# Retention with a mixture of adapters on one core: state per 64 tokens, another beginning, and deferred stores

## The chip, the core and the metric

The kernel runs on one core of one Trainium2 chip. The metric is the device time of one execution in microseconds (us). Times of "before" are from three runs; the profile is of one more execution.

## What is computed

`q`, `k` and `v` have the shape (8 batches, 8 heads, 576 positions, 64). Cut to what matters, the reference is

```python
scores = (1/8) * q @ k.T                         # per batch and head
Dmat = where(rel >= 0, gamma_h ** rel, 0)        # rel = query position - key position
x = (scores * Dmat) @ v                          # all heads side by side: 4608 x 512
logits = x @ w_gate                              # 8 experts
w = softmax of the 2 largest logits, 0 elsewhere
out = x + sum_e w[:, e] * (x @ A[e]) @ B[e]      # A[e]: 512 x 16, B[e]: 16 x 512
```

Because the decay is a power of the distance, `x` of a chunk of positions is the sum of the causal product within the chunk and of `q` times a state, the sum of `k` (outer) `v` over all earlier chunks. The kernel scales by powers of gamma on the key's side (table `gv`) and on the query's side (tables `gx`), so that the state needs no decay of its own.

## The kernel before

**Units.** A unit is 128 positions of two batches, with all heads. Four batches make a quad: four chunks of 128 for two pairs of batches, and one last unit of 64 positions of four batches, the tail unit. There are two quads, so 18 units, 0 to 17; units 8 and 17 are tail units. Units u and u+2 follow each other in the positions of one pair of batches.

**Products of a unit.** `T_mm` transposes k and q on TensorE, 16 products each (`pt_k`, `pt_q`; L248). The causal triangle of 128 positions is cut in halves of 64: `S0_mm` makes the scores of the first 64 keys against all 128 queries (16 products, N=128, L322), `S1_mm` those of the last 64 keys against the last 64 queries (16, N=64, L304). VectorE multiplies both with the triangle (`S0_mask`, `S1_mask`). `O_mm` (16 products, N=128, L432) multiplies a stacked weight W, which has v of the first 64 positions in one half of the partitions and the state in the other, with M, which stacks masked scores and q. `O1_mm` adds the last 64 keys (16, N=64, L451). `U_mm` makes the unit's own k (outer) v over its 128 positions (16 products, K=128, N=64, L395), and `U_out` adds the old state to it, half on VectorE and half on ScalarE and GpSimd (POOL).

**The adapters.** `xT_out` scales the output by `gx` on VectorE; `Z_mm` (8 products, N=136, L487) gives the projections on all A and the logits; `route_a`, `route_s` and `route_b` choose and weigh two experts on VectorE and ScalarE; `X_mm` turns the weighed projection (fp16, L587), `zT_out` copies it, `Y_mm` (L605) multiplies with B, `B_mm` (L620) adds x by transposing it back, `osb_out` copies the sum to `osb`, and `store` writes 2 x 256 KB.

**Order.** All order is written by hand: the order in the code is the order in each engine's queue. Units 0 and 1 and the start of unit 2 are written out. Then the loop `for r in range(2, END)` makes a round of unit r: U of r+1, O of r, scores of r+1, X of r-1, Z and routing of r, transposes of r+2, and Y, B and the store of r-1. Scaling k with `gv` (`k_scale`, L226), laying v into W (`W_values`) and turning q (`q_turn`) are POOL's.

**Loads.** q, k and v come as 2 x 256 KB a unit in runs of 256 bytes, all from the SP queue, except k of unit 0. `freed(u, nm)` issues the load that takes over the buffer of unit u; q has 3 buffers, k and v 4. The stores stand in the same queue, `store(r-1)` in round r; `osb` has 3 buffers.

Of the kernel before, what the change touches and what calls it, by code (L numbers as in the profile page):

```python
# [17 lines left out]
HALF = (LO, HI)  # L18
# [3 lines left out]
def kernel(  # L22
# [26 lines left out]

# [12 lines left out]
    tri3_np = np.stack([tri_np, np.ones((128, 64)), tri_np], axis=1)  # L62


    NG0 = 8
    g0_np = np.zeros((128, 2, HP, NG0), dtype=np.float32)
    gw = [w for w in (8, 16, 32, 64) if w >= NG0]
    gw_np = np.zeros((128, len(gw), 2, HP), dtype=np.float32)
    for hp in range(HP):
        for ho in range(2):  # L70
            g = gam[2 * hp + ho]
            g0_np[HALF[ho], 0, hp, :] = g ** -rows[None, :NG0]
            g0_np[HALF[ho], 1, hp, :] = scale * g ** rows[None, :NG0]
            for x, w in enumerate(gw):
                gw_np[HALF[ho], x, 0, hp] = g ** -float(w)
                gw_np[HALF[ho], x, 1, hp] = g ** float(w)
# [6 lines left out]
    dr_tri = nc.inline_tensor(tri3_np.astype(np.float32), "c_tri")  # L83
# [13 lines left out]
    pack = cpool.tile([128, 256], FP32, tag="pack", name="pack")  # L97
    g0, gws, gv, gc = (pack[:, ends[x] : ends[x + 1]] for x in range(4))
    g0 = g0.rearrange("p (t a i) -> p t a i", t=2, a=HP)
    gws = gws.rearrange("p (x t a) -> p x t a", x=len(gw), t=2)  # L100
    gv = gv.rearrange("p (c h) -> p c h", c=NCH)
    gc = gc.rearrange("p (c h) -> p c h", c=NCH - 1)
    tri3 = cpool.tile([128, 4, 64], FP32, tag="tri3", name="tri3")
    gkx = cpool.tile([128, 2, HP, 128], FP32, tag="gkx", name="gkx")
    gk = gkx[:, 0]
    gx = [gkx[:, 1]] + [
        cpool.tile([128, HP, 128], FP32, tag=f"gx{c}", name=f"gx{c}") for c in range(1, NCH)
    ]
# [27 lines left out]
    NBUF = {"q": 3, "k": 4, "v": 4}  # L136
# [43 lines left out]

    def copy(eng, out, in_):
        if eng is nc.scalar:
            nc.scalar.copy(out=out, in_=in_)  # L183
        else:
            eng.tensor_copy(out=out, in_=in_)  # L185
# [8 lines left out]
    def heads(tl, p):  # L194

        v4 = tl.rearrange("p (b a o) d -> p b a o d", b=2, o=2)
        return [v4[:, b, :, p ^ b, :] for b in range(2)]

    def W_open(u):
        n = 1 if full(u) else 2  # L200
        st[u]["W"] = [
            wk.tile([128, 2, 2, HP, Dh], FP32, tag=f"W{x}", name=f"W{x}", bufs=(5, 2)[x])
            for x in range(n)
        ]
        if units[u][0] == 0:
            for p in range(2):
                nc.gpsimd.memset(st[u]["W"][0][HALF[p], p], 0.0)

    def W_values(eng, u, ps=(0, 1)):
        vt = nat[("v", u)]  # L210
        for x, w in enumerate(st[u]["W"]):
            for p in ps:
                for b, src in enumerate(heads(vt[HALF[x]], p)):
                    copy(eng, w[HALF[1 - p], p, b], src)

    def V1_copy(eng, u):

        s = st[u]
        s["V1"] = wk.tile([64, 2, HP, Dh], FP32, tag="V1", name="V1", bufs=2)
        for b, src in enumerate(heads(nat[("v", u)][HI], 0)):  # L220
            copy(eng, s["V1"][:, b], src)

    def k_scale(eng, u, bs=slice(0, 2)):
        c = units[u][0]
        kt = nat[("k", u)].rearrange("p (b h) d -> p b h d", b=2)[:, bs]
        eng.tensor_tensor(  # L226
            out=kt, in0=kt,
            in1=gv[:, c, :].unsqueeze(1).unsqueeze(3).broadcast_to(
                (128, bs.stop - bs.start, H, Dh)
            ),  # L230
            op=ALU.mult,
        )

    def T_open(u, nm, tag):
        s = st[u]
        s["p" + nm] = bank(tag, [128, 2, HP, 2, 64], name=f"pt_{nm}")
        if nm == "q":
            s["M"] = wk.tile([128, 2, 2, HP, 128], FP32, tag="M", name="M", bufs=3)
            s["Qs"] = wk.tile([128, HP, 2, 64], FP32, tag="Qs", name="Qs", bufs=2)
        else:  # L240
            s["kT"] = wk.tile([128, 2, HP, 2, 64], FP32, tag="kT", name="kT", bufs=2)

    def T_mm(u, nm, bs=(0, 1)):
        src, ps = nat[(nm, u)], st[u]["p" + nm]
        for hp in range(HP):
            for b in bs:
                for r in range(2):
                    mm(  # L248
                        ps[:, r, hp, b, :],
                        lhsT=src[HALF[r], b * H + 2 * hp : b * H + 2 * hp + 2, :],  # L250
                        rhs=ident[HALF[r], 64 * r : 64 * r + 64],
                        is_transpose=True,
                        start=True,
                        stop=True,
                    )

    def q_out(eng, u, p):

        s = st[u]
        copy(  # L260
            eng,
            s["M"][HALF[p], p, 0].rearrange("p a (r i) -> p r a i", r=2),
            s["pq"][HALF[p], :, :, 0, :],
        )

    def qs_out(eng, u):

        s = st[u]
        copy(eng, s["Qs"].rearrange("p a r i -> p r a i"), s["pq"][:, :, :, 1, :])

    def q_turn(eng, u, p):

        s = st[u]
        copy(
            eng, s["M"][HALF[p], p, 1],
            s["Qs"][HALF[1 - p]].rearrange("p a r i -> p a (r i)"),
        )

    def k_out(eng, u, bs=slice(0, 2)):
        s = st[u]  # L280
        if bs == slice(0, 2):
            copy(
                eng, s["kT"].rearrange("p r a b i -> p (r a b i)"),
                s["pk"].rearrange("p r a b i -> p (r a b i)"),
            )
        else:
            copy(eng, s["kT"][:, :, :, bs.start, :], s["pk"][:, :, :, bs.start, :])


    def Q_of(u, b, ho, hp, sl):  # L290
        s = st[u]
        if b == 0:
            return s["M"][HALF[ho], ho, 0, hp, sl]
        return s["Qs"].rearrange("p a r i -> p a (r i)")[HALF[ho], hp, sl]

    def S1_mm(u, tag="R"):

        s = st[u]
        s["ps1"] = bank(tag, [128, 2, 512], name="ps1")
        for hp in range(HP):  # L300
            for b in range(2):
                for ho in range(2):
                    p = ho ^ b
                    mm(  # L304
                        s["ps1"][HALF[p], b, 64 * hp : 64 * hp + 64],
                        lhsT=s["kT"][HALF[ho], 1, hp, b, :],
                        rhs=Q_of(u, b, ho, hp, HI),
                        start=(hp == 0),
# [4 lines left out]
    def S0_mm(u, tag="S"):  # L313

        s = st[u]
        s["ps0"] = bank(tag, [128, 2, HP, 128], name="ps0")
        for hp in range(HP):
            for x, sl in ((0, slice(0, 128)),) if full(u) else ((0, LO), (1, HI)):
                for b in range(2):
                    for ho in range(2):  # L320
                        p = ho ^ b
                        mm(  # L322
                            s["ps0"][HALF[1 - p], b, hp, sl],
                            lhsT=s["kT"][HALF[ho], x, hp, b, :],
                            rhs=Q_of(u, b, ho, hp, sl),
                            start=(hp == 0 and x == 0),
# [4 lines left out]
    def S0b_mm(u, b, tag):  # L331

        s = st[u]
        s.setdefault("ps0b", {})[b] = bank(tag, [128, HP, 128], name="ps0")
        for hp in range(HP):
            for ho in range(2):
                p = ho ^ b
                mm(
                    s["ps0b"][b][HALF[1 - p], hp, :],
                    lhsT=s["kT"][HALF[ho], 0, hp, b, :],  # L340
                    rhs=Q_of(u, b, ho, hp, slice(0, 128)),
                    start=(hp == 0),
                    stop=True,
                    skip_group_check=True,
                )

    def S0b_mask(u, b):
        s = st[u]
        for p in range(2):
            sl = HALF[1 - p]  # L350
            m = tri3[sl, 0:2, :].rearrange("p t i -> p (t i)")
            nc.vector.tensor_tensor(
                out=s["M"][sl, p, b], in0=s["ps0b"][b][sl],
                in1=m.unsqueeze(1).broadcast_to((64, HP, 128)), op=ALU.mult,
            )

    def S1_mask(u):
        s = st[u]
        s["S1"] = wk.tile([128, 2, HP, 64], FP32, tag="S1", name="S1", bufs=2)
        nc.vector.tensor_tensor(  # L360
            out=s["S1"],
            in0=s["ps1"][:, :, 0 : 64 * HP].rearrange("p b (a i) -> p b a i", a=HP),
            in1=tri3[:, 0, :].unsqueeze(1).unsqueeze(1).broadcast_to((128, 2, HP, 64)),
            op=ALU.mult,
        )

    def S0_mask(u, p, bs=slice(0, 2)):
        s = st[u]
        sl = HALF[1 - p]
        n = bs.stop - bs.start  # L370
        if full(u):
            m = tri3[sl, 0:2, :].rearrange("p t i -> p (t i)")
            nc.vector.tensor_tensor(  # L373
# [720 lines left out]
```

## Time and profile before

| | before |
|---|---|
| median of three runs (lowest, highest) | 182.95 us (181.15, 183.76) |
| the profiled execution | 183.94 us |
| its span | 182.2 us |
| TensorE busy (its weight loads) | 173.1 us (157.8) |
| VectorE, ScalarE, GpSimd busy | 128.8, 76.3, 125.1 us |
| moved by DMA | 39.00 MB, 214 GB/s on the mean |
| from HBM, to HBM | 29.09 MB, 9.44 MB |

The span reaches from the first to the last instruction; the execution's time is 1.74 us longer. Busy times of different engines overlap. A row of a group reads: line, engine, operation, output and input tiles, shape, count, then busy time, mean ns of one, idle time ahead and what ended it.

### The profile page before, as it was taken

Reading aid. Unit: us, or ns where it says so; the run is one execution under the profiler, and the core shown is the slowest. Engines: PE = TensorE matmul, PEld = TensorE weight load, DVE = VectorE, ACT = ScalarE, POOL = GpSimd, SP = SyncE. Lnnn points to the kernel's source line nnn. Section 1 sums busy time; section 2 is a strip of 40 time slices with the busy share of each in tenths; the row PEclk is TensorE's granted clock in tenths of the full one; section 3 lists DMA queues with packets and bytes.
Section 4 is the critical chain, followed back from the end, with each engine's and each line's share of the span. In section 5 each row is a group of like instructions: output and inputs, shape, how many; then the busy total and the mean of one; then the engine's idle time right before and its main releaser. Section 6 shows DMA issues by size and latency. Waiting matters only on the chain.

```text
span 182.2 us, 9356 instructions
## 1 busy us (share of the span) xinstructions
PE 173.1 (95%) x4126; PEld 157.8 (87%) x4126; DVE 128.8 (71%) x232; ACT 76.3 (42%) x156; POOL 125.1 (69%) x214
## 2 busy tenths in 40 slices
PE   7998999599999999999999999999999999999980
PEld 6797998498999899998999999999999999989960
DVE  4494763718686869696868596969696969687770
ACT  0734164910707070706273634343444444443330
POOL 7396984998297959796987747858677777792000
PEclk9999999969999999999999999999999999999997
DMA  4999899899997979999989798989999999923125
GB/s 115 288 229 211 182 199 206 181 235 227 219 286 175 255 176 267 219 288 230 270 185 271 173 293 193 258 183 246 220 286 232 264 202 271 273 84 119 55 107 189
DMA packets 119368, 39.00 MB, mean 214 GB/s; under 512 B 114320, under 2 KB 114720, under 8 KB 119328
## 3 DMA queue, kind: packets, MB, share of 16 engines
q1 hardware_dynamic: 116480, 37.30, 82.9%
q10 hardware_dynamic: 2672, 0.96, 2.1%
q8 instruction: 32, 0.52, 1.1%
q0 software_dynamic: 176, 0.15, 0.5%
q14 instruction: 8, 0.07, 0.1%
HBM read 29.09 MB, written 9.44 MB: 212 GB/s over the span
## 4 chain that ended last, share of the span: by engine, by line
PE 87%; POOL 4%; DMA 3%; SPq 2%; DVE 0%; issue 0%; DVEq 0%
PE pz L487 18%; PE px L432 17%; PE pu L395 9%; PE ps L322 8%; PE pt_k L248 5%; PE px L451 5%; PE po L620 5%; PE pt_q L248 4%; PE po L605 4%; PE ps L304 4%; PE pf L723 3%; DMA v<-in_v_dram 3%; SPq L142 2%; PE pzt L587 2%; POOL sel L503 2%; PE pa L514 1%
## 5 line engine op out<-in xcount | busy, mean ns | idle before, releaser
L373 DVE TENSOR_TENSOR M<-ps,tri 64x1024 f32<-64x1024 f32 (+1 forms) x34 | 37.3, 1097 | 3.8 <-PE ps L322 3.1
L487 PE MATMUL pz<-AW,xT 128*128 128x136 f32 x288 | 37.7, 284 | 0.0
L226 POOL TENSOR_TENSOR k<-k,pack 128x1024 f32<-128x1024 f32 (+1 forms) x18 | 32.5, 1806 | 6.6 <-PE pt_k L779 2.9
L185 POOL COPY M<-Qs 64x512 f32<-64x512 f32 x36 | 21.9, 609 | 21.9 <-ACT Qs L183 16.1
L432 PE MATMUL px<-M,W 128*64 128x128 f32 (+1 forms) x640 | 36.1, 268 | 0.0
L185 POOL COPY W<-v 64x256 f32<-64x256 f32 x78 | 29.2, 395 | 10.0 <-DMA v<-in_v_dram 6.8
L487 PEld LDWEIGHTS pz<-AW,xT 128*128 128x128 f32 x288 | 34.6, 190 | 0.4
L183 ACT COPY kT<-pt_k 128x1024 f32<-128x1024 f32 x17 | 17.2, 1015 | 40.1 <-PE pt_k L248 40.1
L432 PEld LDWEIGHTS px<-M,W 128*64 128x64 f32 x640 | 32.8, 141 | 0.2
L470 DVE TENSOR_TENSOR xT<-px,gx 128x1024 f32<-128x1024 f32 x11 | 13.5, 1225 | 17.8 <-PE px L451 13.4
L185 DVE COPY osb<-po 128x1024 f32<-128x1024 f32 (+2 forms) x18 | 19.2, 1075 | 5.9 <-PE po L620 5.0
L596 ACT COPY zT<-pzt 128x256 f16<-128x256 f16 (+1 forms) x19 | 6.9, 361 | 37.7 <-PE pzt L587 37.7
L183 ACT COPY M<-pt_q 64x512 f32<-64x512 f32 x35 | 20.2, 577 | 1.8 <-DVE M L185 0.7
L395 PE MATMUL pu<-v,k 128*64 128x64 f32 x512 | 19.2, 229 | 1.6 <-DMA v<-in_v_dram 1.6
L395 PEld LDWEIGHTS pu<-v,k 128*64 128x64 f32 x512 | 16.8, 141 | 3.0 <-ACT kT L183 1.4
L322 PE MATMUL ps<-Qs,kT 64*64 64x128 f32 (+1 forms) x304 | 17.9, 259 | 0.0
L322 PE MATMUL ps<-M,kT 64*64 64x128 f32 (+1 forms) x304 | 17.9, 259 | 0.0
L188 POOL TENSOR_TENSOR W<-pn,W 64x512 f32<-64x512 f32 x12 | 15.2, 1270 | 0.9
L322 PEld LDWEIGHTS ps<-M,kT 64*64 64x64 f32 x304 | 14.8, 134 | 0.2
L322 PEld LDWEIGHTS ps<-Qs,kT 64*64 64x64 f32 x304 | 14.8, 134 | 0.0
L248 PEld LDWEIGHTS pt_k<-ident,k 64*128 64x128 f32 x272 | 9.8, 138 | 3.7 <-issue 2.5
L248 PE MATMUL pt_k<-ident,k 64*128 64x64 f32 x272 | 12.1, 229 | 0.5 <-POOL k L226 0.5
(73 smaller groups left out, 295.7 us busy)
## 6 DMA issues: line engine op xcount, KB each, us to landing
q<-in_q_dram SPq DMA_DIRECT2D x36, 256.0 KB, 5.2
v<-in_v_dram SPq DMA_DIRECT2D x36, 256.0 KB, 4.7
k<-in_k_dram SPq DMA_DIRECT2D x34, 256.0 KB, 4.7
out_dram<-osb SPq DMA_DIRECT2D x34, 256.0 KB, 4.6
k<-in_k_dram ACTq DMA_DIRECT2D x2, 256.0 KB, 4.9
An<-in_moe_A_dram SPq DMA_DIRECT2D x1, 256.0 KB, 5.4
out_dram<-osb ACTq DMA_DIRECT2D x2, 128.0 KB, 2.8
out_dram<-osb SPq DMA_DIRECT2D x2, 128.0 KB, 2.9
```

The source lines that it names most:

```text
L183: nc.scalar.copy(out=out, in_=in_)
L185: eng.tensor_copy(out=out, in_=in_)
L188: eng.tensor_tensor(out=out, in0=a, in1=b, op=ALU.add)
L226: eng.tensor_tensor(out=kt, in0=kt, in1=gv[:, c, :].unsqueeze(1).unsqueeze(3).broadcast_to((128, bs.stop - bs.start, H, Dh)), op=ALU.mult,)
L248: mm(ps[:, r, hp, b, :], lhsT=src[HALF[r], b * H + 2 * hp : b * H + 2 * hp + 2, :], rhs=ident[HALF[r], 64 * r : 64 * r + 64], is_transpose ...
L322: mm(s["ps0"][HALF[1 - p], b, hp, sl], lhsT=s["kT"][HALF[ho], x, hp, b, :], rhs=Q_of(u, b, ho, hp, sl), start=(hp == 0 and x == 0), stop=True,
L373: nc.vector.tensor_tensor(out=s["M"][sl, p, bs].rearrange("p b a i -> p (b a) i"), in0=s["ps0"][sl, bs].rearrange("p b a i -> p (b a) i"), ...
L395: mm(s["pu"][HALF[p], b, hp, :], lhsT=nat[("k", u)][:, h, :], rhs=nat[("v", u)][:, h, :], start=(hp == 0 and b == 0), stop=True, skip_grou ...
L432: mm(s["pxb"][b][HALF[ho], hp, sl], lhsT=s["W"][x][:, p, b, hp, :], rhs=s["M"][:, p, b, hp, sl], start=(hp == 0 and x == 0), stop=True, sk ...
L451: mm(s["px"][HALF[ho], b, hp, HI], lhsT=vv, rhs=s["S1"][HALF[p], b, hp, :], start=False, stop=True, skip_group_check=True,)
L470: nc.vector.tensor_tensor(out=s["xT"][:, bs].rearrange("p b a i -> p b (a i)"), in0=s["px"][:, bs].rearrange("p b a i -> p b (a i)"), in1= ...
L487: mm(s["pz"][:, n, :], lhsT=s["xT"][:, n, dt, :], rhs=AW[:, dt, :], start=(dt == 0), stop=(dt == HP - 1), skip_group_check=True,)
```

## The change

- **Scores.** One kind of product, 64 keys against their own 64 queries: `S_mm`, 32 products of 64x64, N=64, for `S0_mm` and `S1_mm`. The part of the last 64 queries against the first 64 keys goes through the state.
- **State per 64 tokens.** The state is carried on in PSUM, one bank for each pair of batches, over a whole quad. `U_mm` adds to it in two parts of K=64: the first half of unit r+1 and the second half of unit r, in one run of 32 products. `U_out` copies the state after each half to the stacked weight V of the next half, once with ScalarE and VectorE, once with ScalarE alone.
- **Output.** `O_mm` is one stacked product for each half, batch and head: 32 of K=128, N=64; `O1_mm`, V1 and S1 are gone.
- **Scaling.** k stays as it was loaded. POOL scales v instead while it lays it into V: four 64x512 products a unit (`V_values`) for one of 128x1024 (`k_scale`) and four to six copies.
- **Copies.** The transposes of k and q leave PSUM in halves, all on ScalarE; `osb_out` is ScalarE's in every round.
- **Banks and order.** PSUM is A0, A1, P0, P1, E0, E1 and the double bank Q. The loop begins at round 0, with another order inside.
- **Beginning.** Masks, transposes and copies of unit 0 are spread over ScalarE and VectorE; the selection matrices of A are made first on POOL; A comes by POOL's queue; the two loads of k of unit 1 are issued by ScalarE.
- **Loads and stores.** k has 5 buffers. Stores are kept back (`kept`, `store_to`): nine units wait in eleven buffers of `osb`, and from round 13 on the rest goes out, 4, 3, 3 and 3 units in four rounds.

```diff
-    NBUF = {"q": 3, "k": 4, "v": 4}
+    NBUF = {"q": 3, "k": 5, "v": 4}
...
+    def V_values(eng, u, r, hos=(0, 1)):
+        c, sl = units[u][0], HALF[r]
+        for ho in hos:
+            eng.tensor_tensor(
+                out=st[u]["V"][r][ho][sl],
+                in0=nat[("v", u)][sl].rearrange("p (b a o) d -> p o a b d", b=2, o=2)[:, ho],
+                in1=gv[sl, c, :] ... .broadcast_to((64, HP, 2, Dh)),
+                op=ALU.mult,
+            )
...
+    def S_mm(u, tags, bs=(0, 1)):
+        ps = two_banks(tags, [128, HP, 2, 64], "ps")
+        for hp in range(HP):
+            for b in bs:
+                for ho, r in ((0, 0), (1, 1), (0, 1), (1, 0)):
+                    mm(ps[ho][HALF[r], hp, b, :],
+                       lhsT=s["kT"][r][HALF[ho], hp, b, :],
+                       rhs=s["M"][r][1 - r][HALF[ho], hp, b, :], ...)
...
+    def U_mm(*parts):
+        for u, r in parts:
+            c, bp = units[u]
+            if c == 0 and r == 0:
+                state[bp] = bank(f"E{bp % 2}", [128, HP, 2, Dh], name="pu")
+        for hp in range(HP):
+            for b in range(2):
+                for ho in range(2):
+                    for n, (u, r) in enumerate(parts):
+                        o = ho ^ n
+                        mm(state[bp][HALF[o], hp, b, :],
+                           lhsT=nat[("k", u)][HALF[r], b * H + 2 * hp + o, :],
+                           rhs=st[u]["V"][r][o][HALF[r], hp, b, :], ...)
...
+                    for r in rr:                       # O_mm
+                        for ho in range(2):
+                            mm(s["px"][b][HALF[ho], hp, 64 * r : 64 * r + 64],
+                               lhsT=s["V"][r][ho][:, hp, b, :],
+                               rhs=s["M"][r][ho][:, hp, b, :], ...)
...
+    LAG = 9
...
+    for r in range(END):
+        nxt, nn = r + 1, r + 2
+        one, two = ("A", "P") if r % 2 == 0 else ("P", "A")
+        ups = [(u, x) for u, x in ((nxt, 0), (r, 1)) if full(u)]
+        if not full(nxt):
+            U_mm(*ups)
+        if r > 0:
+            for b in range(2):
+                O_mm(r, (b,), one)
+                xT_out(r, b)
+        S_mm(nxt, (two + "0", two + "1") if r > 0 else "Q")
+        if r > 0:
+            X_mm(r - 1, one + "1")
+            zT_out(r - 1)
+        for u in late:
+            U_out(both, u, 1)
...
+        Z_open(r, one + "0")
+        Z_mm(r)
+        for x, ho in ((0, 0), (0, 1), (1, 0)):
+            S_mask(nxt, x, ho)
+        route_a(r)
+        route_s(r)
+        S_mask(nxt, 1, 1)
+        route_b(r)
+        if r > 0:
+            Y_mm(r - 1)
+        V_values(nc.gpsimd, nxt, 1)
+        if nn < NU:
+            V_open(nn)
+            V_values(nc.gpsimd, nn, 0)
+        late = []
+        if full(nxt):
+            U_mm(*ups)
+            U_out((nc.scalar, nc.vector), nxt, 0)
+            late = [r] if full(r) else []
+        if nn < NU:
+            T_open(nn, "k", two)
+            T_mm(nn, "k")
+            for x in range(2):
+                k_out(nc.scalar, nn, x)
+        if r > 0:
+            B_mm(r - 1)
+        freed(r, "k")
+        freed(nxt, "v")
+        if nn < NU:
+            T_open(nn, "q", one)
+            T_mm(nn, "q")
+            freed(nn, "q")
+            for x in range(2):
+                q_out(nc.scalar, nn, x)
+            for x in range(2):
+                q_turn(nc.gpsimd, nn, x)
...
+        if r > 0:
+            osb_open(r - 1)
+            osb_out(nc.scalar, r - 1)
+            kept.append(r - 1)
+            store_to(min(LAG, LAG * (END - 1 - r) // 4))
```

More of the change, by code (lines that the diff above doesn't have):

```diff
@@ L404, in U_out @@
-    def U_out(u):
-        s = st[u]
-        us, x = behind(u)
-        if "W" not in st[us]:
-            W_open(us)
-        new, old = st[us]["W"][x], s["W"][0]
-        if units[u][0] == 0:
-            for p in range(2):
-                copy(nc.scalar, new[HALF[p], p], s["pu"][HALF[p]])
-            return
-        add(nc.vector, new[LO, 0], s["pu"][LO], old[LO, 0])
-        pn = wk.tile([128, 2, HP, Dh], FP32, tag="pn", name="pn", bufs=2)
-        copy(nc.scalar, pn[HI], s["pu"][HI])
-        add(nc.gpsimd, new[HI, 1], pn[HI], old[HI, 1])
@@ L739 @@
     load_batch(0, "q", 1)
[L740 removed]
+    nc.scalar.dma_start(out=tri, in_=dr_tri.ap())
     nc.vector.memset(warm, 0.0)
@@ L1024, in of @@
+    pzs = [bank(f"E{n}", [128, 2, ER + E], name="pz") for n in range(2)]
     def of(n):
```

642 lines of the change are left out of this document (193 added, 449 removed).

## The prediction

> **What bounds the kernel now.** I read the page first, then the chain of waits in order of time, then the busy times by stretch, then the groups by shape.
>
> ```profile
> span 182.2 us, 9356 instructions
> PE 173.1 (95%) x4126; PEld 157.8 (87%) x4126; DVE 128.8 (71%) x232; ACT 76.3 (42%) x156; POOL 125.1 (69%) x214
> PE 87%; POOL 4%; DMA 3%; SPq 2%; DVE 0%; issue 0%; DVEq 0%
> ...
> 107.28:116.32 9.04, 9.04 (x232) 8.38 (x234) 7.08 (x13) 3.91 (x8) 6.71 (x11) 1.00 0.91 223
> ```
>
> The last row is one round of the steady part: TensorE is busy for all of its 9.04 us at clock 1.00; VectorE 7.08, ScalarE 3.91, GpSimd 6.71, the DMA engines 0.91 with 223 GB/s. So a round costs what its products cost, and the chain shows them one behind the other:
>
> ```profile
> 92.30 1.87 PE px L432 x64
> ...
> 108.94 1.08 PE pu L395 x32
> 110.02 1.75 PE px L432 x32
> 111.77 0.62 PE px L451 x32
> 112.86 0.88 PE ps L322 x32
> 113.95 1.93 PE pz L487 x16
> 116.32 0.65 PE pt_k L248 x16
> 116.97 0.51 PE po L620 x16
> 117.48 0.51 PE pt_q L248 x16
> 117.98 1.08 PE pu L395 x32
> ...
> 165.93 0.93 PE ps L322 x64
> ```
>
> (Start, length, what; one fp32 product is two records, a transpose one.) From 108.94 to 117.98 the pieces add up to the round: states 1.08, first output product 1.75, second 0.62, small scores between 112.39 and 112.86 0.47, large scores 0.88, the fp16 turn X between 113.74 and 113.95 0.21, router and adapters Z 1.93, Y between 115.88 and 116.32 0.44, and three transposes 0.65, 0.51, 0.51. Where the tile form of TensorE changes, some 0.2 of idle is in these pieces:
>
> ```profile
> PEld px L451 <- issue: 2.7, 16, 0.2
> PEld pt_k L248 <- issue: 2.5, 12, 0.2
> PEld L587 <- issue: 2.1, 12, 0.2
> ```
>
> **The round after.** Removed: 16 products each of L432 (N=128), L451, L304, L322 and L395; POOL's scaling of k and its copies. Added: 32 score products, 32 output products, 32 state products, all with N=64. X, Z, Y and the transposes stay.
>
> Scores: 32 products on 64x64 quarters, N=64. The round with a tail unit has this shape: 64 records in 0.93 (row at 165.93), plus 0.17 for O to S, the idle that now sits ahead of L451: 1.10, for 0.47+0.88.
> Outputs: 32 products of 128 rows by 64 columns, N=64. The tail unit has them: 64 records in 1.87 (row at 92.30), for 1.75+0.62.
> States: 32 products with K=64 on quarters; no row of L395 has that. From below they go like the scores, 0.93; from above at today's pace of 1.08 for 32 records, 2.16 for 64. I take 0.93, since their order also walks all four quarters, with 0.2 idle ahead (Y to U).
> Tk keeps 0.65; its 0.2 idle may fall away or stay. Sum: 1.87 + 1.10 + 0.21 + 1.93 + 0.44 + 1.13 + 0.65 + 0.51 + 0.51 = 8.35; without Tk's idle 8.15. I take 8.3 against 9.04.
>
> The trace shows idle at three of today's four changes of form and none from the q transposes to the states (117.48 + 0.51 meets 117.98), so I charge none from them to O. The Trainium skill (TensorEngine Tiling (Array Packing), Key Properties) says that every change of tiling mode drains the engine. By it the fifth change would cost 0.2 more and the time would be some 2.6 us longer; the trace does not agree at that one place.
>
> **What has to hide beside 8.3 us.**
>
> ```profile
> L373 DVE TENSOR_TENSOR M<-ps,tri 64x512 f32<-64x512 f32 x8 | 5.5, 689 | 3.3 <-PE ps L322 3.1
> L465 DVE TENSOR_TENSOR xT<-px,gx 128x512 f32<-128x512 f32 x6 | 4.0, 686 | 2.2 <-PE px L451 2.2
> L545 DVE MAX8 m<-pz 128x8 f32<-128x8 f32 x36 | 4.3, 154 | 1.7 <-PE pz L487 1.7
> L563 DVE SCALAR_TENSOR_TENSOR cm<-pz,m,sg 128x8 f32<-128x8 f32 x36 | 6.4, 218 | 1.2 <-ACT sg L555 1.2
> L575 DVE TENSOR_TENSOR zc<-pz,cm 128x256 f16<-128x256 f32 x17 | 7.2, 424 | 0.6
> L188 DVE TENSOR_TENSOR W<-pu,W 64x512 f32<-64x512 f32 x12 | 8.1, 675 | 2.4 <-PE pu L395 2.4
> L183 ACT COPY Qs<-pt_q 128x512 f32<-128x512 f32 x17 | 10.0, 585 | 0.4
> L183 ACT COPY osb<-po 128x1024 f32<-128x1024 f32 x2 | 2.0, 1012 | 1.4 <-PE po L620 1.4
> L226 POOL TENSOR_TENSOR k<-k,pack 128x512 f32<-128x512 f32 x2 | 2.1, 1040 | 2.9 <-PE pt_k L779 2.9
> L226 POOL TENSOR_TENSOR k<-k,pack 128x1024 f32<-128x1024 f32 x16 | 30.4, 1902 | 3.6 <-DMA k<-in_k_dram 2.4
> L185 POOL COPY M<-Qs 64x512 f32<-64x512 f32 x36 | 21.9, 609 | 21.9 <-ACT Qs L183 16.1
> L188 POOL TENSOR_TENSOR W<-pn,W 64x512 f32<-64x512 f32 x12 | 15.2, 1270 | 0.9
> ```
>
> VectorE: 2 xT at 0.69, 4 masks at 0.69, one state copy 0.68, the router's pieces 0.31, 0.44, 0.42 and a small one of some 0.2: 6.2. ScalarE: today's 3.91, two more copies of 0.58 (three halves of states for one) and osb, until now VectorE's, 1.01: 6.1. POOL: two turns at 0.61 and four scalings of v, 64x512 with a broadcast factor. That form is new: from 0.61 (a copy) to 1.27 (an add of the same size); the same scaling with 512 elements took 1.04, which I take: 5.4, at most 6.3. All are under 8.3.
>
> Each can still be late. Count from O's first product: O ends at 1.87, S at 2.97, Z at 5.1, Y at 5.55, U at 6.7, Tk at 7.3, B 7.8, Tq 8.3. Tk writes the banks that hold the scores, so it now waits for the fourth mask, which stands on VectorE behind the router's maximum, which waits for Z: 5.1 + 0.1 + 0.5 + 0.7 = 6.4. Tk would start at 6.7, 0.3 later: the thinnest cover of the round. Behind Tk stand B, Tq and the next O. Tq's banks come free with zc at about 7.1. The k copies on ScalarE (two of 0.58 from 7.4) free the next O's two banks at 8.0 and 8.6, and the halves of O want them at 8.3 and 9.2. The q copies end at 9.7, osb at 10.8; the next S wants q at 10.2, the next zT at 11.5. POOL turns q up to 10.5, which is 2.2 into the next round, and then scales v until 6.4; O wants that at 8.3.
>
> **Loads.** All bytes stay. Stores leave the first ten rounds, and SP's loads no longer stand behind stores that wait for osb; what remains is 1.57 MB of loads a round.
>
> ```profile
> 6.21 2.58 SPq L142 DMA_DIRECT2D k<-in_k_dram  x2
> ...
> 31.47 3.83 SPq L142 DMA_DIRECT2D k<-in_k_dram  x2
> ...
> 15.00:20.00 5.00, 4.52 (x113) 4.22 (x114) 2.57 (x4) 2.68 (x5) 3.38 (x15) 1.00 0.80 181
> ...
> 134.42:143.46 9.04, 9.04 (x232) 8.38 (x234) 7.08 (x13) 3.91 (x8) 7.05 (x11) 1.00 1.02 258
> ...
> 161.07:169.43 8.36, 8.36 (x204) 7.50 (x206) 6.66 (x12) 3.45 (x7) 4.06 (x10) 1.00 0.17 65
> ```
>
> Between the two SP rows the queue was never free and passed nine loads of 0.524 MB and a half one: 4.98 MB in 25.26 us, 197 GB/s, or 7.98 us a unit; the slowest 5 us gave 181, or 8.69. So loads hide under 8.3, with 4% to spare. With one unit's stores a round, in rounds 10 to 12, 253 GB/s is wanted; the row at 134.42 gave 258. The other thirteen units' stores, 6.8 MB, fall into the last four rounds, 33 us, when all loads are issued: 206 GB/s, and stores alone ran at 65 GB/s with 0.17 of the engines' time. Nothing waits for them but the end.
>
> **The beginning and the end.**
>
> ```profile
> 18.19 1.03 PE ps L322 x32
> ...
> 30.54 5.65 DMA v<-in_v_dram
> 36.24 1.54 PE pu L395 x28
> ...
> 47.00 1.08 PE pu L395 x32
> ...
> 163.41 1.90 PE px L432 x32
> ```
>
> Now round 3 starts at 47.00, after a stall for v of unit 3, which landed at 36.19. The new beginning takes k's scaling and the choice of A's copies out of POOL's chain, and asks ScalarE for k of unit 1 late. With unit 1's scores 2 us later than today's 18.19 for that, round 0 (8.3 less O, X and Y, 5.8) and rounds 1 and 2 end at 42.6 by the products alone. But the transposes of round 2 need q of unit 4: 1.55 MB behind that v in the order of loads, at 197 GB/s 7.9 us later, 44.1. With the transposes 44.7, a gain of 2.3.
>
> From round 3 to 16 are 13 rounds. Today they take 163.41 - 47.00 = 116.4. After: 11 at 8.3 and two beside the tail unit, which have one of the two state products, at 7.9: 107.1, a gain of 9.3. From there to the end is 182.2 - 163.4 = 18.8, and stays but for one half state product, an estimate of 0.3 from the 0.47 and 0.93 above with the saved outputs.
>
> Sum: 44.7 + 107.1 + 19.1 = 170.9 of span. The profiled execution took 183.94, 1.74 around its span: 172.6. It stands 0.5% above the median of 182.95, so on the scale of the runs some **172**, 6% less.
>
> **Rivals.**
> The fourth mask comes late. For it: 0.3 of cover, and each handover from VectorE to TensorE is only guessed at 0.1. Against: VectorE has 2 us free a round. If 0.3 a round comes out, 13 x 0.3 more: 176.
> Loads set the pace, and the change does for TensorE what it says without the time following. For it: 4% to spare, and the 181 GB/s of one stretch. Against: the prefetch is three rounds deep. At 181 throughout, 13 x 8.69 = 113.0, q of unit 4 at 44.8 and so round 3 at some 45.4: 45.4 + 113.0 + 19.1 + 1.7 = 179.2, less 0.9: 178. Below 179 GB/s it is no change.
> The quarters do not overlap, so that it becomes slower: U's pairs take k straight from the loads and v from scaled tiles, into banks that stay open over rounds. If U and S ran as two lanes, like 64 records in 1.87, each costs 0.94 more: 8.3 + 1.9 = 10.2, 13 x 1.9 = 24.7 more, 197; for U alone 184. It makes the kernel slower from 1.1 us a round above my sum. Against it: the scores at 165.93 are such quarters at 0.93. The Trainium skill (TensorE: Matmul & The Clock Gate, LDWEIGHTS) states that a weight load costs by its columns, whatever K, which would make halving K a loss; the trace's loads of 64 columns are indeed as long for 64 rows as for 128, but overlap.
>
> **How the numbers follow.** Forecast 0.60 (166 to 176 by its bounds 8.15 and 8.6 a round and 2 us at the beginning), late mask 0.18, loads 0.15 (at 181 GB/s or less), lost overlap 0.07. What can be told from no change is 2%: under 179.3 is faster. The forecast, the late mask and half of the loads' case are faster, 0.85; the other half, 0.08, the same; 0.07 slower. The range is 166 to 180: the forecast's own from below, the loads' case at some 178 GB/s from above; lost overlap is left out.
>
> **What would show it.** Right: rounds of 8.1 to 8.5 us with TensorE busy throughout; the scores x64 near 0.93, the states x64 near 0.95, the outputs x64 near 1.9; round 3 near 45; the DMA share near 0.85 with some 190 GB/s until round 10, then stores. Wrong: idle ahead of the k transposes with a mask as releaser (late mask), waits for loads at V or at the transposes in each round (loads), states near 1.9 (lost overlap), or an end later than 20 us after the last round's first output product, from stores that still wait.

## The result, and the profile after

The changed kernel takes 209.95 us (median of 4, 209.78 to 211.41) against 183.35 for the kernel before in the same comparison: a ratio of 1.151, 95% interval 1.139 to 1.164. It is 15% slower. The forecast was 172.0 with a range up to 180, and neither a rival nor the range held it. Every ratio below is to the kernel before in the same comparison; its median was 183.35 here and 185.55 to 186.08 in the later ones, so versions from different comparisons are better compared by ratio than by median. Some executions of every version are slower than the rest; medians are of all of them, ratios of the fast ones alone.

First the page of the changed kernel: span, engines, the granted clock in tenths of full speed (40 slices of the span), the queue that fetches instructions, and the chain by engine.

```profile
span 208.3 us, 10430 instructions
PE 174.2 (84%) x4646; PEld 158.5 (76%) x4646; DVE 117.0 (56%) x259; ACT 99.2 (48%) x202; POOL 105.0 (50%) x138
...
PEclk9985699999999999999999999999999999879996
...
q8 instruction: 36, 0.59, 1.2%
...
PE 79%; issue 10%; DVE 3%; DMA 3%; SPq 2%; ACT 0%; ACTq 0%; DVEq 0%
```

TensorE is busy for 174.2 us, as before (173.1), but in a span that is 26.1 longer. Before, "issue" (the engine waits for nothing that the profile shows) was 0% of the chain; now it is 10%. The chain of one round, in order of time:

```profile
133.90 2.02 PE px L340 x64
135.92 0.97 PE ps L275 x56
136.89 1.30 issue
138.19 0.34 PE ps L275 x8
138.53 0.22 PE pzt L460 x2
138.75 1.91 PE pz L363 x16
140.66 0.44 PE po L478 x4
141.10 1.09 PE pu L313 x64
142.19 0.65 PE pt_k L246 x16
142.83 0.51 PE po L493 x16
143.34 0.77 issue
144.10 0.71 PE pt_q L246 x16
144.82 2.02 PE px L340 x64
146.84 0.85 PE ps L275 x47
147.69 1.44 issue
```

Outputs 2.02, states 1.09, Z 1.91, Y 0.44, the transposes 0.65, 0.51 and 0.51: the pieces cost what the forecast said, to 0.15 us. But the round from 133.90 to 144.82 takes 10.92, with two holes of 1.30 and 0.77. They stand in the middle of a row of like products: the scores are cut behind 56 of 64 records, and one round later behind 47. A cause in the data would stand at the same product each round; this one moves through the code.

Next the chain's shares by line over the 13 rounds from round 3 (52.76) to round 16 (190.01), and the row of the round shown above from the stretches by time:

```profile
by line: PE px L340 19.4%; PE pz L363 18.8%; issue 13.6%; PE ps L275 13.0%; PE pu L313 11.1%; PE pt_k L246 6.6%; PE pt_q L246 5.3%; PE po L493 5.1%; PE po L478 3.8%; PE pzt L460 2.3%; DVE M L291 0.5%; DVE ns L420 0.4%; DVE m L418 0.2%
...
133.90:144.82 10.92, 8.86 (x264) 8.06 (x266) 5.93 (x13) 5.60 (x11) 5.31 (x6) 1.00 0.82 205
```

137.25 us are 10.56 a round, where 8.3 was forecast and 8.96 is what the kernel before takes. Against 13 x 8.35 = 108.6, the sum of the pieces, 28.7 are too many. Of 137.25, 13.6% or 18.7 are the holes; the scores have 13.0% or 17.8 instead of 14.3 (+3.5; beside a hole they take longer, 0.97 + 0.34 = 1.31 in the round above for 1.09 undisturbed), the outputs 26.6 instead of 24.3 (+2.3), VectorE's part 1.5, small amounts the rest. Part of that is the clock: in the last of these rounds, behind its largest hole of 2.02, the granted clock was 0.87 and Z took 2.65 instead of 1.91.

The whole difference of the spans, 26.1, is then: rounds 3 to 16 137.25 - 116.4 = +20.9; the beginning 52.76 - 47.00 = +5.8; the end 18.3 - 18.8 = -0.5.

The beginning has a cause of its own, seen in the chain and in the stretches by time:

```profile
10.77 3.82 DMA v<-in_v_dram
...
14.61 0.44 ACTq L133
...
15.10 0.37 ACT M L181
...
10.00:15.00 5.00, 0.00 (x0) 0.00 (x0) 1.88 (x5) 0.00 (x0) 3.54 (x3) 0.88 1.14 259
15.00:20.00 5.00, 4.21 (x62) 3.87 (x64) 1.52 (x4) 1.45 (x4) 0.00 (x0) 0.50 1.19 269
20.00:25.00 5.00, 5.00 (x98) 4.58 (x97) 0.41 (x1) 2.24 (x4) 0.00 (x0) 0.59 1.05 238
```

ScalarE stands at the issue of its load of k of unit 1 until a load of v has landed, 14.59, though that load has nothing to do with v: the program makes it wait for the load that stands eight places ahead of it in the program's order of loads, so that no more than eight are under way. The copies of M behind it, and all of TensorE, wait with it (no TensorE work from 10 to 15). After that idle the granted clock is 0.50 and 0.59 for 10 us, and the products take nearly twice as long.

### The profile page after: what moved, and what is told of

It is laid out like the page before. It is cut to its first block, busy times and chain, and to the rows that moved or that the text cites. A ratio compares the mean times of both kernels' runs of the same rounds, so it can differ in the third digit from the quotient of the medians.

```text
span 208.3 us, 10430 instructions
## 1 busy us (share of the span) xinstructions
PE 174.2 (84%) x4646; PEld 158.5 (76%) x4646; DVE 117.0 (56%) x259; ACT 99.2 (48%) x202; POOL 105.0 (50%) x138
## 4 chain that ended last, share of the span: by engine, by line
PE 79%; issue 10%; DVE 3%; DMA 3%; SPq 2%; ACT 0%; ACTq 0%; DVEq 0%
PE px L340 18%; PE pz L363 17%; PE ps L275 11%; PE pu L313 9%; PE pt_k L246 6%; PE pt_q L246 5%; PE po L493 4%; PE po L478 3%; SPq L133 2%; PE pzt L460 2%; DMA v<-in_v_dram 2%; DMA pack<-c_pack 1%; PE pf L606 1%; PE pa L390 1%; DVE M L291 1%
## 5 line engine op out<-in xcount | busy, mean ns | idle before, releaser
L210 POOL TENSOR_TENSOR V<-v,pack 64x512 f32<-64x512 f32 x69 | 70.9, 1046 | 5.8 <-DMA v<-in_v_dram 3.2
L291 DVE TENSOR_TENSOR M<-ps,tri 64x512 f32<-64x512 f32 (+1 forms) x76 | 48.5, 658 | 31.5 <-PE ps L275 30.4
L183 POOL COPY M<-M 64x512 f32<-64x512 f32 x34 | 21.1, 619 | 80.8 <-ACT M L181 79.8
L353 DVE TENSOR_TENSOR xT<-px,gx 128x512 f32<-128x512 f32 x36 | 24.8, 691 | 41.3 <-PE px L340 41.2
L275 PE MATMUL ps<-M,kT 64*64 64x64 f32 x1152 | 25.2, 229 | 19.4 <-issue 13.0
L340 PE MATMUL px<-M,V 128*64 128x64 f32 x1152 | 39.6, 227 | 0.4 <-issue 0.4
L340 PEld LDWEIGHTS px<-M,V 128*64 128x64 f32 x1152 | 36.6, 141 | 2.0 <-issue 0.5
L275 PEld LDWEIGHTS ps<-M,kT 64*64 64x64 f32 x1152 | 21.2, 140 | 22.3 <-issue 14.3
L181 ACT COPY V<-pu 64x512 f32<-64x512 f32 x49 | 28.4, 580 | 11.0 <-PE pu L313 5.9
L181 ACT COPY M<-pt_q 128x512 f32<-128x512 f32 (+1 forms) x36 | 19.0, 577 | 12.5 <-DMA v<-in_v_dram 7.0
L313 PEld LDWEIGHTS pu<-V,k 64*64 64x64 f32 x1024 | 19.2, 137 | 3.4 <-issue 3.0
L313 PE MATMUL pu<-V,k 64*64 64x64 f32 x1024 | 21.7, 224 | 0.0
```

What stands on the lines that cost most here:

```text
L210: eng.tensor_tensor(out=st[u]["V"][r][ho][sl], in0=nat[("v", u)][sl].rearrange("p (b a o) d -> p o a b d", b=2, o=2)[:, ho], in1=gv[sl, c, ...
L275: mm(ps[ho][HALF[r], hp, b, :], lhsT=s["kT"][r][HALF[ho], hp, b, :], rhs=s["M"][r][1 - r][HALF[ho], hp, b, :], start=(hp == 0 and b == bs[0]),
L291: nc.vector.tensor_tensor(out=to, in0=ps, in1=tri[HALF[r]].unsqueeze(1).broadcast_to((64, HP if b is not None else 2 * HP, 64)), op=ALU.mult,)
L313: mm(state[bp][HALF[o], hp, b, :], lhsT=nat[("k", u)][HALF[r], b * H + 2 * hp + o, :], rhs=st[u]["V"][r][o][HALF[r], hp, b, :], start=(c = ...
L340: mm(s["px"][b][HALF[ho], hp, 64 * r : 64 * r + 64], lhsT=s["V"][r][ho][:, hp, b, :], rhs=s["M"][r][ho][:, hp, b, :], start=(hp == 0 and r ...
L353: nc.vector.tensor_tensor(out=xT, in0=s["px"][b], in1=gx[units[u][0]], op=ALU.mult)
```

## The experiments

**The theory.** Instructions reach TensorE over a DMA queue of their own (q8), in packets of 16 KB that hold 256 instructions. A matmul record is two instructions, weight load and product. The kernel before has 8252 such instructions and 32 packets, the changed one 9292 and 36. In the trace a hole stands at every border of 256 instructions where the next packet landed late, and TensorE resumes 1.25 to 1.6 us after the landing (mean 1.41). With the semaphore instructions of TensorE's queue counted too, 17 of the changed kernel's 18 holes of more than 0.5 us between 45 and 190 us stand behind the same remainder of 256, 193 or 194. So the theory is: the next block is asked for only after a border, and a block whose products are shorter than the fetch stops TensorE. A round has 264 records after (528 instructions, 2.06 blocks) and 232 before (1.81 blocks). **The rivals:** the order of the work or the waits in it; the loads; the deferred stores.

**The number of instructions alone**, in the kernel before: O's N=128 products cut in two of N=64, so that all else stays; then S0's as well.

```diff
@@ O_mm
-                for x, sl in ((0, slice(0, 128)),) if full(u) else ((0, LO), (1, HI)):
+                for x, sl in ((0, LO), (1, HI)):
...
-                            lhsT=s["W"][x][:, p, b, hp, :],
+                            lhsT=s["W"][0 if full(u) else x][:, p, b, hp, :],
@@ S0_mm (second run only)
-            for x, sl in ((0, slice(0, 128)),) if full(u) else ((0, LO), (1, HI)):
+            for x, sl in ((0, LO), (1, HI)):
...
-                            lhsT=s["kT"][HALF[ho], x, hp, b, :],
+                            lhsT=s["kT"][HALF[ho], 0 if full(u) else x, hp, b, :],
```

> The kernel before, with each first output product of N=128 cut into two of N=64 (32 instead of 16 a round, the same result). TensorE's array work hardly grows: 64 records in 1.87 us instead of 32 in 1.75, so +0.12 us a round, but a round now has as many TensorE instructions as the changed kernel (some 530 instead of 466). Theory 'instructions': TensorE stalls at the border of each block of 256 instructions, for the next block has not landed; then this kernel gets stalls of 1 to 2 us too, rounds of some 10.3 us and a time near 203 us. Rival 'order': the stalls come from the waits of the new order; then no stalls, 185 us.

> As e1, and the large score products cut in two as well (some 594 instructions a round, array work +0.17 us). 'Instructions': at about 256 instructions in 5 us a round is 11.5 us, the time 220 us. 'Order': 186 us.

Measured: 190.52 us, ratio 1.022 (1.013 to 1.033), and 206.71, ratio 1.112 (1.102 to 1.122). Waits of the second:

```profile
PEld ps L322 <- issue: 10.8, 9, 2.3
PE ps L322 <- issue: 9.9, 9, 2.2
```

The kernel before, in its own order and with its own loads and stores, gets the changed kernel's holes once it has its instructions. This rules out the order of the work as what makes them. The first run is near the edge of what can be told from no change, the second is clear of it. The size was overrated, 203 and 220 having been expected (185 and 186 by the rival): a block that is long enough costs nothing, and with the first cut alone only the dense blocks fell short.

**The changed kernel without most loads, with fewer instructions, and with both.** First the loads that take over a buffer are left out. Then the state products are halved (16 of N=128, over both batches with the first batch's k). Then both.

```diff
@@ load  (first and third run)
+        if u >= NBUF[nm]:
+            nat[(nm, u)] = nat[(nm, u % NBUF[nm])]
+            return
@@ U_mm  (second and third run)
-            for b in range(2):
-                for ho in range(2):
...
-                            state[bp][HALF[o], hp, b, :],
-                            lhsT=nat[("k", u)][HALF[r], b * H + 2 * hp + o, :],
+                        state[bp][HALF[o], hp].rearrange("p b d -> p (b d)"),
+                        lhsT=nat[("k", u)][HALF[r], 2 * hp + o, :],
```

> The changed kernel without the loads that would take over a buffer (every unit beyond the first buffers computes on old data); stores stay, all in the last four rounds. The queues are empty from about 25 to 110 us. If the blocks of instructions come late because they queue behind loads: no stalls there, rounds of 8.45 us, and stalls again once the stores run; time near 190 us. If the block's own time is enough to stall TensorE, or the stalls are waits of the order: rounds of 10 us as before, 205 us or more.

> The changed kernel with 16 state products of N=128 instead of 32 of N=64 (both batches take the first batch's k, so the state of the second is another). The array streams as many columns, but a round has 64 instructions less (some 460 instead of 524). 'Instructions': rounds of 9 to 9.2 us, time near 190 us. 'Order': the columns and the waits are the same, so 207 to 210 us.

> The changed kernel with both cuts at once: the loads that take over a buffer are left out (as in the run without them), and the state update is 16 products with N=128, over both batches with the first batch's k (32 records a round fewer). Theory 'instruction blocks' (256 TensorE instructions come as one 16-KB block; TensorE stalls when the block has not been there for 1.4 us at the border): without loads the block's start falls from 2.4 to some 1.4 us after the border, transfer 1.1, then 1.4, 3.9 in all, against some 5.0 us of work in a block. So the stalls go, a round costs what its products cost, some 8.45 us, and rounds 3 to 16 take 110 instead of 137 us: 184 to 187 us. Rival 'the order of the work': each cut gave 11 us for a reason of its own and stalls of another kind remain; 193 to 199 us.

Measured: 198.12 (ratio to the kernel before 1.066, 1.052 to 1.080), 198.83 (1.058, 1.045 to 1.071) and 191.77 (1.041, 1.031 to 1.050). Each cut gives back 11 to 12 us by the medians, or 0.085 and 0.093 of the ratio, and both together 18 us, or 0.111. All three times lie between those of the theory and of the rival. A round of the third and the start of the next, from its chain, and a row of its waits:

```profile
116.56 2.02 PE px L342 x64
118.57 1.09 PE ps L278 x64
119.67 0.22 PE pzt L462 x2
119.88 1.92 PE pz L365 x16
121.83 0.26 DVE m L420 x2
122.11 0.68 DVE ns L422
122.83 0.70 DVE M L294
123.67 0.68 PE pt_k L249 x15
124.34 0.51 PE po L495 x16
124.85 0.51 PE pt_q L249 x16
125.36 2.02 PE px L342 x64
...
PE pt_k L249 <- DVE M L294: 3.8, 11, 1.4
```

Loads and instruction count together account for nearly all holes: three are left on the chain from round 3 on, 1.9 us, where the changed kernel has 18.6. Rounds 3 to 16 take 118.9 us, not the 110 expected. The round shown is 8.80, not 8.45, since without the holes the fourth mask is late after all: Z ends at 121.80, the mask at 123.53, 1.73 later, where Y and U cover 1.5. That is the lateness of the forecast's own first rival. What makes it is one small instruction of the router, `ns`. The rows of this run, and then those of the changed kernel in the round from 133.90:

```profile
118.62 4.16 POOL L213 TENSOR_TENSOR V<-v,pack 64x512 f32<-64x512 f32 x4
122.11 0.68 DVE L422 SCALAR_TENSOR_TENSOR ns<-m 128x2 f32<-128x2 f32 x1
...
135.94 4.16 POOL L210 TENSOR_TENSOR V<-v,pack 64x512 f32<-64x512 f32 x4
140.98 0.16 DVE L420 SCALAR_TENSOR_TENSOR ns<-m 128x2 f32<-128x2 f32 x1
```

In the changed kernel POOL's multiplies of V are over at 140.10, `ns` takes 0.16, and the mask ends 1.20 after Z. Without the holes Z comes while POOL still multiplies, and `ns` takes 0.68 and ends 0.01 after the last multiply. In 11 of the 13 rounds it takes 0.61 to 0.85 and ends at most 0.03 after a multiply; in the changed kernel it takes 0.34 or more in 4 of 13. That VectorE stands there because of POOL is read from these ends; no run moves POOL's work away.

**Blocks by themselves.** In one run, behind the last product of the kernel before stand 24 blocks of score products with N=64 and 6 with N=256, and 8 MB of loads run beside the first of them.

```diff
+    for u in [x for x in range(NU) if full(x)]:
+        load_open(u, "q")
+        for b in range(2):
+            load_batch(u, "q", b)
+    ps = bank("S", [128, 2, HP, 128], name="ps0")
+    for n, wide in ((48, 64), (12, 256)):
+        for x in range(n):
+            for i in range(32):
+                ho, b = i % 2, (i // 2) % 2
+                mm(
+                    ps[HALF[1 - (ho ^ b)], b].rearrange("p a i -> p (a i)")[:, 0:wide],
+                    lhsT=se["kT"][HALF[ho], 1, i // 4 % HP, 0, :],
+                    rhs=se["M"][HALF[ho], ho, 0].rearrange("p a i -> p (a i)")[:, 0:wide],
+                    start=True, stop=True, skip_group_check=True,
+                )
```

> The kernel before, and behind its last product a measurement of instruction blocks by themselves, whose results nobody reads: 1536 score products on 64x64 quarters with N=64 (24 blocks of 256 TensorE instructions; operands stay where they are, no semaphore between them), beside the first of which 8 MB of loads run again (some 40 us), and then 384 such products with N=256 (6 blocks). By the scores of the kernel before (64 records in 0.93 us, N=64; 32 in 0.88, N=128) the products alone take 1.9 us a block, and some 7 us with N=256. Theory 'a block lands too late': TensorE stops at each border, and a block takes what the others showed: some 2 to 2.4 + 1.1 + 1.4 = 4.5 to 4.9 us while the loads run, 1.4 + 1.1 + 1.4 = 3.9 us when they have ended, and 7 us without a stop for N=256. Rival 'the products' order or their waits': no stops here, 1.9 us a block throughout, 46 us for the first 24. Rival 'the loads alone hold the blocks up': 4.5 and more beside the loads, some 2 us without them.

From its chain, and its stretches by time (us; TensorE busy and records; weight loads; VectorE, ScalarE, POOL; clock; DMA share; GB/s):

```profile
187.58 2.09 PE ps L1072 x128
189.67 2.73 issue
...
248.44 2.09 PE ps L1072 x128
250.53 1.64 issue
...
PE ps L1072 <- issue: 39.0, 24, 2.7
...
189.40:220.16 30.76, 18.38 (x912) 17.30 (x906) 0.00 (x0) 0.00 (x0) 0.00 (x0) 0.83 0.92 206
228.99:265.18 36.19, 20.92 (x1296) 19.58 (x1291) 0.00 (x0) 0.00 (x0) 0.00 (x0) 1.00 0.02 5
280.00:300.00 20.00, 20.00 (x376) 18.82 (x372) 0.00 (x0) 0.00 (x0) 0.00 (x0) 1.00 0.01 2
```

This is the theory with nothing else in it: 128 records (256 instructions), a hole, 128 records, a hole. The first stretch is 7 blocks, 4.39 us each at 206 GB/s beside them, where the products of a block take 2.6 at a granted clock of 0.83; the second 10 blocks, 3.62 us each with nothing beside them, where the products take 2.09. With N=256 a block has 6.8 us of work (376 records in 20 us) and there is no hole. Both rivals named there fall; "some 2 us without loads" falls by 1.6 us. The Trainium skill (Runtime: NRT & Kernel Launch, Instruction fetch mechanics) states that the next block is fetched while the current one runs and that crossing a border is "mostly hidden". Here that holds for the block of 6.8 us and not for the one of 2.09.

From the packets' times and the borders in each trace (a border found by the count of weight loads, to some 0.3 us; before, where no hole marks it, to some 0.5), means in us from 45 to 165, or in the last two rows over the two stretches above. A hole is here the idle time ahead of a weight load at a border; on the chain, which goes by the ends of products, the same stretches have less: 3.9, 12.5, 16.0, 6.8 and 1.9 us in pieces over 0.15, in the order of the rows from the second on.

| kernel | border to packet's start | transfer | landed to resumed | products in a block | sum of holes |
|---|---|---|---|---|---|
| before | 1.4 | 1.0 | - | 4.96 | 0 |
| before, O cut | 2.1 | 1.2 | 1.4 | 4.49 | 6.2 |
| before, O and S0 cut | 2.1 | 1.1 | 1.4 | 4.09 | 15.8 |
| after | 2.4 | 1.06 | 1.41 | 4.27 | 18.7 |
| after, no loads | 1.8 | 1.1 | 1.4 | 4.28 | 10.1 |
| after, both cuts | 1.5 | 1.17 | 1.35 | 4.95 | 1.3 to 2.7 |
| alone, beside loads | 1.91 | 1.11 | 1.39 | 2.6 | |
| alone | 1.20 | 1.09 | 1.36 | 2.1 | |

The changed kernel needs 2.4 + 1.06 + 1.41 = 4.9 us a block and has 4.27 of products on the average, 3.2 in its densest. At 2.06 blocks 4.9 make a round of some 10.0; measured, 10.56. The kernel before, at 1.81 blocks, comes to 8.9 with the same 4.9, and to 6.9 with its own row and the others' 1.4: its 8.96 stood above this limit, by 0.1 to 2 us, unseen.

**Fewer instructions without loss of work.** Eight transposes over all 128 rows (N=128) for sixteen over 64, in the changed kernel and in the one before, and Y as two products for four.

```diff
@@ T_mm  (B_mm and Y_mm likewise; the copies behind them follow the new layout)
-        for hp in range(HP):
-            for b in range(2):
-                for r in range(2):
-                    mm(
-                        ps[r][:, hp, b, :],
-                        lhsT=src[HALF[r], b * H + 2 * hp : b * H + 2 * hp + 2, :],
-                        rhs=ident[HALF[r], 64 * r : 64 * r + 64],
+        for b in range(2):
+            for hp in range(HP):
+                mm(
+                    ps[b][:, hp, :],
+                    lhsT=src[:, b * H + 2 * hp : b * H + 2 * hp + 2, :],
+                    rhs=ident,
```

> The changed kernel with transposes over all 128 rows: 8 instead of 16 products for k, for q and for the way back of x, and Y in two products of N=512 instead of four of 256 (the same result). 52 instructions less a round, 472 for 524, and the array's own time stays about the same (8 of about 60 ns for 16 of 32 ns). 'Instructions': fewer and longer blocks, 1.84 a round instead of 2.05; rounds of 9.3 to 9.7 us and a time of 193 to 197 us. 'Order': 207 to 210 us.

> The kernel before with the same wide transposes and Y (412 instructions a round for 464). It has no stalls at block borders to lose; what may go is the 0.2 us of idle where TensorE's form changes from Y to the transposes, and a little per transpose: 0.2 to 0.4 a round, 178 to 180 us. If wide transposes are slower than pairs of halves: 184 to 187 us.

Measured: 205.20 (1.108, 1.099 to 1.118) and 196.08 (1.058, 1.049 to 1.066). The first lies between the two forecasts; the second is slower than the kernel before, which no theory had. From the chain of the first:

```profile
113.92 0.87 PE po L495 x8
114.80 0.87 PE pt_q L248 x8
```

Eight wide transposes take 0.87 where sixteen of half the rows take 0.51: the narrow ones start in pairs, one pair every 63 ns, and the wide ones one by one, every 109. With the transposes of k (0.87 for 0.65) that is 0.94 a round. The kernel before, which had no holes to lose, lost 10.5 us by it and has rounds of 10.00 for 9.04. The changed kernel gains by fewer holes, 3.0 us on the chain of rounds 3 to 16 for 18.6, and the wide transposes eat most of that: its rounds take 10.0 instead of 10.56.

**The beginning and the stores.** k of unit 1 loaded from SP, so that ScalarE does not stand at its issue; and each store issued at once.

```diff
@@ first run
+    load(1, "k")
     load(1, "q")
...
-    load_open(1, "k")
-    load_batch(1, "k", 0, nc.scalar)
...
-    load_batch(1, "k", 1, nc.scalar)
@@ second run
-            store_to(min(LAG, LAG * (END - 1 - r) // 4))
+            store_to(0)
```

> The changed kernel with both loads of k of unit 1 issued by SP ahead of q of unit 1, instead of by ScalarE. 'Queue slots': ScalarE's load waits until the eighth load before it has landed and holds ScalarE's copies from 8.1 to 14.6 us, TensorE runs dry and its clock is halved from 16 to 24 us; without it TensorE is not idle there, the clock stays, round 3 begins 5 to 7 us earlier, and the time is near 203 us. Rival 'data': the beginning waits for the bytes of k and v anyway, 209 us.

> The changed kernel with each unit's store issued in its own round, as before, out of the same eleven buffers. If the nine rounds of loads without stores lengthen the way of the instruction blocks (2.4 us from border to start instead of 1.6), that falls back towards 1.8 and the time to some 203 us. If deferring is harmless: 209 to 211 us. If it does help: 213 us or more, with waits for loads.

Measured: 208.22 (1.119, 1.106 to 1.133) and 212.68 (1.144, 1.131 to 1.156). In the first, the outputs of rounds 2 and 3 begin at

```profile
36.86 2.02 PE px L340 x64
47.08 2.02 PE px L340 x64
```

so round 3 begins 5.7 us earlier than in the changed kernel: the wait at the issue was the cause of the late beginning. But rounds 3 to 16 then take 141.5 instead of 137.25, and 4.3 of it are given back; the holes on their chain add up to 21.5 instead of 18.6. Why they grow was not settled. So the time came out near the rival's 209, though the rival's reason falls. Stores at once change nothing that can be told: the ratio is within the interval of the changed kernel's, and rounds 3 to 16 take 137.2. The blocks still start 2.6 after a border, not 1.8, so the deferred stores are not what delays them.

**Smaller loads, and another order in the kernel before's beginning.** Each load of 256 KB as two of 128 KB in the changed kernel; and in the kernel before, in round 2, O and the turn of x ahead of U, over the wait for v of unit 3.

```diff
@@ load_batch, after
-            out=nat[(nm, u)][:, b * H : (b + 1) * H, :],
...
+                out=nat[(nm, u)][:, b * H + 4 * x : b * H + 4 * x + 4, :],
...
+            for x in range(2)
@@ loop, before
+        if r == 2:
+            O_mm(r)
+            O1_mm(r)
+            freed(r, "v")
+            xT_out(r)
         if full(nxt):
             U_mm(nxt, "E" if r > 2 else "F")
```

> The changed kernel with each load of 256 KB issued as two of 128 KB (the same bytes, twice the issues). Only eight loads are under way from an engine's queue at a time, so half the bytes stand queued on the DMA engines when a block of instructions is asked for. If the blocks start late because they stand behind queued load packets, the time from border to start falls from 2.4 to some 1.9 us, the stalls by a third, and the time to 200 to 205 us. If it is not what is queued but that a load is under way at all, no change, 209 to 211. If the smaller loads move fewer bytes a second, the rounds wait for loads: above 213.

> The kernel before with one edit in its beginning: in round 2 the output products and the turn of x of unit 2 stand ahead of the state products of unit 3, not behind them, so that they cover the wait for v of unit 3 (TensorE idle for some 2.1 us between 34 and 36 us, and a granted clock of 0.66 behind it). If that idle is on the chain, round 3 begins some 3 us earlier: 0.98 to 0.985 of the kernel before. If the loads behind it (q of unit 4) set the begin of round 3 anyway, the same time, 0.995 to 1.005.

Measured: 216.59 (1.167, 1.147 to 1.187) and 186.35 against 185.97 (1.001, 0.993 to 1.008, 12 and 17 runs). The smaller loads do not bring the blocks earlier: border to start is 2.4 on the mean, as in the changed kernel, and rounds 3 to 16 take 135.6. In the execution that was profiled, of 213.35 us, the time is lost in the beginning, where round 3 starts at 57.41 instead of 52.76, and not by waits for loads in the rounds. So halving the size of a load does not help; that loads run at all is what goes with a later start (1.91 for 1.20 by themselves, 2.4 for 1.8 in the changed kernel). Why the start varies from 1 to 4 us within one trace stays open. The other order leaves the time as it was, as the second forecast had it, but not for the reason given there: in the execution that was profiled, a long one of 188.75 us, round 3 begins with U at 45.01 instead of 47.00, and no product waits for q of unit 4. The rounds behind it then wait for v, five times and 2.3 us in all. Whether that is so in the shorter executions too stays open. No version here beats the kernel before.

## Why the prediction was wrong

**The step that failed** is the first: "So a round costs what its products cost". It was read from a TensorE busy for all of its 9.04 us, and it was true of that kernel; the change then added 32 records (64 instructions) to a round and took 0.5 us of products out, without a term for what brings instructions. The missing term is 10.56 - 8.35 = 2.2 us a round, 1.4 of it holes. The row that held it was on the page of the kernel before and looked like nothing with 1.1% of the DMA engines' time:

```profile
q8 instruction: 32, 0.52, 1.1%
```

**The sum of the pieces was right.** 8.35 was forecast, 8.45 is what undisturbed pieces give: outputs 2.02 for 1.87, scores 1.09 for 1.10, states 1.09 for 0.93 and 0.2, the transposes of k 0.65 and of q 0.51, as forecast. The quarters do overlap, and the lost-overlap rival, the only one on the slow side, fell at U x64 in 1.09.

**The late mask** was a rival at 0.18. In the round of the changed kernel shown above it is not late, 1.20 us from Z's end to the fourth mask's where 1.3 was forecast; without the holes it is, 1.73, since the router's pieces ahead of it then take 1.0 and not 0.5. The working had 0.7 us for the mask and 0.5 for the router, and no term for a VectorE instruction that lasts until POOL's multiply ends. So even without any hole, an estimate from the run with both cuts (118.9 less 1.9 of holes for 13 rounds) is 52.76 + 117.0 + 18.3 + 1.7 = 190: no gain.

**The beginning** was forecast to end at 44.7 and ended at 52.76. "Asks ScalarE for k of unit 1 late" was priced at 2 us for unit 1's scores; these began at 27.50 instead of 18.19, 9.3 later. ScalarE stood at the issue some 6.5 us, for which there was no term, and the clock halved behind the idle stretch. With the load on SP it is 47.08: no gain, and no loss.

**The loads** did not set the pace (0.82 of the engines' time at 205 GB/s, no waits for them in the rounds), but they cost in a place that the forecast did not look at: a block's start is 0.6 to 0.7 us later beside them. The end was 18.3 for 19.1.

## What to carry to other kernels

Count instructions as well as product time: in these runs 256 TensorE instructions needed some 4.4 to 4.9 us of work beside running loads (3.6 without), or TensorE stopped at the border. The small products (64x64 quarters, N=64) ran at 1.9 to 2.1 us per 256 and could not be fed at that pace for long, so halving N or K for the same work was no gain here, where TensorE is the bound. The sign in a profile is "issue" idle of 1 to 2 us that falls on another product every round. And the engine that issues a DMA can stand at the issue itself.

## What was not expected of the hardware

A fetched block is usable 1.35 to 1.41 us after its packet has landed, on the mean of each kernel. Its fetch begins 1.2 us after a border with idle DMA engines, and 1.9 to 2.4 beside loads, though its queue is its own. ScalarE stood 6.5 us at the issue of a load, for the landing of another one eight places ahead. A VectorE instruction on 128x2 numbers takes 0.16 us, and took 0.61 to 0.85 in 11 rounds where a POOL multiply ran beside it. The wide fp32 transposes cost 109 ns each and the narrow ones 32, so the same data moved in half the instructions took 1.7 times as long.
